# Moving loads between queues and waits in the prologue of a fused state-space and feed-forward kernel

## The chip, the cores and the metric

The kernel runs on one core of a Trainium2 chip. The metric is device time in microseconds (us), start to end of one execution; a run's number is the median of several executions. TensorE (PE) multiplies matrices, VectorE (DVE) and ScalarE (ACT) work on SBUF and PSUM, GpSimd (POOL) works on SBUF. SyncE (SP), ScalarE and GpSimd also issue DMAs, each into a queue of its own.

## The reference

Two stages. The first is a chunked linear recurrence over a sequence, for 4 batches and 8 heads, 768 tokens, head size 32 and state size 16; the second a bilinear feed-forward layer over its output, with model width 256 and inner width 1536.

```python
log_a = np.log(np.clip(a, 1e-06, 1.0))
for c in range(nc):                      # chunks of 32 tokens
    cum = np.cumsum(la, axis=-1)
    L = np.exp(cum[:, :, :, None] - cum[:, :, None, :]) * causal
    M = np.einsum('bhin,bhjn->bhij', Cc, Bc) * L
    y_intra = np.einsum('bhij,bhjd->bhid', M, xc)
    y_inter = np.einsum('bhin,bhnd->bhid', Cc, state) * np.exp(cum)[:, :, :, None]
    y[:, :, sl] = y_intra + y_inter
    state = decay_full * state + np.sum(Bx, axis=2)   # Bx = B x, decayed to the chunk's end
...
x = attn_out.transpose(0, 2, 1, 3).reshape(B * S, H * D)     # 3072 tokens x 256
return ((x @ w_a) * (x @ w_b)) @ w_out
```

Inputs and output are float32.

## The kernel before

**Tiling.** The kernel uses blocks of 128 tokens (six of them) instead of the reference's chunks of 32. A block has four batches, worked in two pairs, so there are twelve pairs p = 0 to 11; pairs 0 and 1 are block 0. VectorE's `scan` turns `a` into running products `Pr`, one block per instruction. Their value in the middle of the block is inverted (`over_mid`, tile `rmid`), and factors for B and C come from `Pr` and `rmid`: for block 0 by small matmuls (`factors_mm`), for blocks 1 to 5 by `mid_rows`, `turned_rows`, `batch_factors` and `batch_inverse`.

**One pair of block 0.** `scale_bc` multiplies B (tile `bm`) and C (tile `cm`) by their factors on VectorE. `transposes` turns both on TensorE, VectorE copies B out (tile `bt`), ScalarE copies C (tile `ct`). `scores` multiplies them into four PSUM banks, `mask` multiplies with the causal table (three quarters on VectorE, one through ScalarE and GpSimd), `pv_u` or `pv1` multiplies the masked scores with x, and the result goes to `X2T` as float16.

**Block 1 (pairs 2 and 3) and later blocks** have B and C loaded by batch (`load_q`, tiles `bq` and `cq`); `scale_q` scales them on GpSimd into `planes`, and `turn` transposes them on VectorE (tile `turned`) for `scores`. `clear` fills the planes with zeros once.

**Feed-forward.** `unit_mm` multiplies two inner columns' worth of weights `Wa` or `Wb` with `X2T`, `evac_a` copies the a-part to SBUF on ScalarE, `times` multiplies it with the b-part on VectorE. `out_mm` multiplies with `Wo`. From block 1 on, `bunit` and `bout` do the same for all four batches at once. Each weight matrix is loaded in two halves by GpSimd (`load_w`, `load_wo`), which converts float32 to float16 on the way.

**Order.** The schedule is written out by hand (`tc.manual_schedule()`): each engine runs its instructions in the order of the program text, and waits only where data or a buffer makes it wait. Feed-forward units stand between the steps of the recurrence so that TensorE has work. `warmup` matmuls, whose results nobody reads, fill TensorE's time in the first microseconds. PSUM banks for the feed-forward come from the string `BANKS`, one digit per call of `bank()`.

**Queues.** The first loads alternate between SyncE and ScalarE. GpSimd issues the x of pair 0, the first halves of Wa and Wb, the x of pair 1 and the second half of Wa in one go; Wb's second half follows later, and Wo's halves at lines 864 and 876. SyncE's loads of block 1 carry an explicit wait on the first half of Wa (tile `w0`, lines 815 and 816). Behind them on SyncE stand the float32 x of pairs 2 and 3 (`load_x32`) and their B (`load2`). `load1` (line 143) loads one batch of one pair, or a part of its partitions if `i0` and `n` are given.

Of the kernel before, what the change touches and what calls it, by code (L numbers as in the profile page):

```python
# [14 lines left out]
ALU = mybir.AluOpType  # L15
PSUM = bass.MemoryType.PSUM
AFTER = mybir.DependencyInfo(mybir.DependencyClass.Sync, mybir.DependencyReason.DATA)
# [2 lines left out]
SS = 64.0  # L20

BANKS = (
    "012313213212312312031203123021032103120312013201320130231021302130231203120312013023102310"
    "2312013201320132012301230123012301230123012301320132013201320132013201320132013201320"
)


# [1 line left out]
def kernel(  # L29
# [113 lines left out]
    def load1(eng, p, which, bt, i0=0, n=64, to=None):  # L143
        blk, bp = divmod(p, NBP)
        if p >= P2:
            return eng.dma_start(
                by_token(pair_in[p][which])[:, bt],
                (B, C, x)[which][2 * bp + bt, :, blk * Q : (blk + 1) * Q, :].rearrange("h q n -> q h n"),
            )
        src = (B, C, x)[which][2 * bp + bt, :, blk * Q + 2 * i0 : blk * Q + 2 * i0 + 2 * n, :]  # L150
        if to is None:
            to = pair_in[p][which]
        return eng.dma_start(
            to[64 * bt + i0 : 64 * bt + i0 + n].rearrange("i h r n -> i h (r n)"),
            src.rearrange("h (i r) n -> i h (r n)", r=2),
        )
# [3 lines left out]
    def load_q(eng, blk, parts=ALL_Q):  # L160
        if blk not in by_batch:
            by_batch[blk] = [inq.tile([128, H, 4, N], f32, name=n_, tag=n_) for n_ in ("bq", "cq")]
        return [
            eng.dma_start(
                by_batch[blk][w][32 * b : 32 * b + 32].rearrange("i h s n -> i h (s n)"),
                (B, C)[w][b, :, blk * Q : (blk + 1) * Q, :].rearrange("h (i s) n -> i h (s n)", s=4),
            )
            for w, b in parts
        ]
# [12 lines left out]
    def load_w(half, W):  # L182
        src = moe_w_a if W is Wa else moe_w_b
        c = slice(half * KC, (half + 1) * KC)
        return nc.gpsimd.dma_start(W[half], src.rearrange("(f p) e -> p f e", p=128)[:, :, c])

    def load_wo(half):
        return nc.gpsimd.dma_start(
            Wo[:, 6 * half : 6 * half + 6].rearrange("p (g kk) e -> p g (kk e)", kk=3),
            moe_w_out.rearrange("(g p kk) e -> p g (kk e)", p=128, kk=3)[:, 2 * half : 2 * half + 2],  # L190
        )
# [6 lines left out]
    load1(nc.scalar, 0, 1, 1)  # L198
    load1(nc.sync, 0, 1, 0, 0, 32)
    load1(nc.scalar, 0, 1, 0, 32, 32)  # L200
    for w in (1, 0):
        load1(nc.sync, 1, w, 0)
        load1(nc.scalar, 1, w, 1)
    nc.scalar.preload_act_table_set("natural_log_exp_and_others")
    nc.vector.memset(zero, 0.0)
    nc.gpsimd.memset(ident, 1.0)
# [21 lines left out]
    for p in range(2):  # L228
        for bt in range(2):
            load1(nc.gpsimd, p, 2, bt)  # L230
        if p == 0:
            w0 = load_w(0, Wa)
            load_w(0, Wb)
    load_w(1, Wa)

    def warmup(bank, *widths):
        for cols in widths:
            nc.tensor.matmul(  # L238
                bank[:, 0:cols],
                nc.const_aps.tensor(1.0, [128, 128], mybir.dt.bfloat16),  # L240
                nc.const_aps.tensor(1.0, [128, cols], mybir.dt.bfloat16),
                start=True,
                stop=True,
                skip_group_check=True,
            )


    def scan(lo, hi):
        for k in range(lo, hi):
            nc.vector.tensor_tensor_scan(Pr[:, k], a_sb[:, k], zero, 1.0, ALU.mult, ALU.add)  # L250

    def over_mid(lo, hi):
        nc.vector.reciprocal(rmid[:, lo:hi], Pr[:, lo:hi, 63])
# [32 lines left out]
    def mid_rows(lo, hi, eng):  # L286
        k = slice(lo + NBLK - NT, hi + NBLK - NT)
        eng.tensor_tensor(
            out=Ps[:, lo:hi], in0=Pr[:, k], in1=rmid[:, k].unsqueeze(2).broadcast_to((BH, hi - lo, Q)), op=ALU.mult
        )  # L290
# [5 lines left out]
    def turned_rows(lo, hi):  # L296
        nc.vector.transpose(
            Pt[:, lo:hi].rearrange("p k s c -> p (k s) c"), Ps[:, lo:hi].rearrange("p k (i s) -> p k s i", s=4)
        )
# [67 lines left out]
    def transposes(p, ps=None, between=None, apart=False):  # L367
        s = st[p]
        if ps is None and apart:
            ps = [SC[0], SC[1]]  # L370
        TB, TC = (TT[:, 0:256], TT[:, 256:512]) if ps is None else [t_.bitcast(f16)[:, 0:256] for t_ in ps]
        for T_, src in ((TB, s["bm"]), (TC, s["cm"])):
            for r in range(2):
                nc.tensor.transpose(
                    T_[:, r * 128 : (r + 1) * 128], src[:, r].rearrange("p h n -> p (h n)"), ident
                )
            if between:
                between()
                between = None
        BT = mid.tile([128, 2, 2, Q], f16, name="bt", tag="bt")  # L380
        CT = mid.tile([128, 2, Q], f16, name="ct", tag="ct")
        co, ci = CT.rearrange("p t q -> p (t q)"), TC
        if p < P2:
            co, ci = CT.rearrange("p t (i r) -> p r (t i)", r=2), TC.rearrange("p (r c) -> p r c", r=2)
        b_ = nc.vector.tensor_tensor(  # L385
            out=BT.rearrange("p e r k -> p e (r k)"),
            in0=TB.unsqueeze(1).broadcast_to((128, 2, 256)),
            in1=par.unsqueeze(2).broadcast_to((128, 2, 256)),
            op=ALU.mult,
        )  # L390
        c_ = nc.scalar.copy(co, ci)
        if apart:
            tc.declare_no_dep(c_.ins, b_.ins.name, reason="reads of two banks")
        if p < P2:
            BT = BT.rearrange("p e r (t i) -> p e r t i", t=2)
        s["BT"], s["CT"] = BT, CT
# [37 lines left out]
    def product0(m2, e):  # L434

        return (
            st[0]["T1"][:, 2 * m2 : 2 * m2 + 2].rearrange("p m (e r) q -> p e m (r q)", e=2)[:, e],
            (SC0, SC1)[m2][:, :, e * 256 : e * 256 + 256],
            causal.rearrange("p r q -> p (r q)").unsqueeze(1).broadcast_to((128, 2, 2 * Q)),
        )  # L440

    def mask(out_in, by_pool=False):
        o_, i_, c_ = out_in
        if by_pool:
            tmp = mid.tile([128, *c_.shape[1:]], f32, name="tmp", tag="tmp")
            nc.scalar.copy(tmp, i_)  # L446
            nc.gpsimd.tensor_tensor(out=o_, in0=tmp, in1=c_, op=ALU.mult)  # L447
        else:
            nc.vector.tensor_tensor(out=o_, in0=i_, in1=c_, op=ALU.mult)  # L449
# [110 lines left out]
    def evac0(u, bt, eng, py):  # L560
        o_, i_ = X2T[:, 0, bt, u], py[bt][:, u * Q : (u + 1) * Q]
        if eng is nc.scalar:
            nc.scalar.activation(out=o_, in_=i_, func=AF.Copy, scale=YS / SS)
        else:
            nc.vector.tensor_scalar(o_, i_, YS / SS, None, ALU.mult)
# [27 lines left out]
    def unit_mm(p, k2, W):  # L593
        ps = bank("aps" if W is Wa else "bps")
        for kk in range(2):
            k = 2 * k2 + kk
            for f in range(2):
                nc.tensor.matmul(  # L598
                    ps[:, kk * 2 * Q : (kk + 1) * 2 * Q],
                    W[k // 6][:, f, k % 6 // 3 * 384 : (k % 6 // 3 + 1) * 384].rearrange("p (c kk) -> p kk c", kk=3)[  # L600
                        :, k % 3
                    ],
                    X2T[:, p, :, f],
                    start=(f == 0),
                    stop=(f == 1),
                    skip_group_check=True,
                )
        return ps
# [175 lines left out]
    scale_bc(0, 1, nc.vector, v.rearrange("p (r b h) -> p r b h", r=2, b=NBP)[:, :, 0])  # L784
    over_mid(1, 2)
    sel_over_mid(1, 2, nc.vector)
    mid_rows(0, 1, nc.gpsimd)
    tb, tcp = bank("tb"), bank("tc")
    transposes(0, [tb, tcp], lambda: warmup(SC[3], 256))
    nc.scalar.copy(flat(fC, 0, 1), v)  # L790
# [3 lines left out]
    mask(product0(0, 0))  # L794
    mask(product0(0, 1))
    mask(product0(1, 1), by_pool=True)
    mask(product0(1, 0))
    clear(planes[0], nc.gpsimd)
    warmup(tcp, 512)
# [5 lines left out]
        evac0(0, bt, nc.scalar, py)  # L805
    warmup(tcp, 512, 128)
    scale_bc(1, 1, nc.vector)
    scan(4, 5)
    scale_bc(1, 0, nc.vector)
    clear(planes[1], nc.gpsimd)  # L810
    pv_u(0, 1, py, True)
    for bt in range(2):
        evac0(1, bt, (nc.scalar, nc.vector)[bt], py)
    load_w(1, Wb)
    for i_ in load_q(nc.sync, 1):
        tc.add_manual_dep(i_.ins, w0.ins.name, AFTER, reason="first weights ahead of block 1")
    for p in (2, 3):
        tiles(p)
    x_in = [load_x32(p) for p in (2, 3)]
    for p in (2, 3):  # L820
        load2(nc.sync, p, 0)
    warmup(tcp, 512, 512)
    transposes(1, apart=True)
    aps = [unit_mm(0, 0, Wa)]
    scan(5, NBLK)
    over_mid(2, NBLK)
    clear(planes[2], nc.gpsimd)
    nc.gpsimd.tensor_tensor(out=hr, in0=Pr[:, 0:NG, Q - 1], in1=rmid[:, 0:NG], op=ALU.mult)
# [32 lines left out]
    nc.scalar.copy(G.rearrange("p g k -> p (g k)"), gps)  # L861
    times(0, 2, bps[2], asb[2])
    turned_rows(0, 1)
    load_wo(0)
    batch_factors(0, 1, *range(nb), eng=nc.gpsimd)
    mid_rows(1, NT, nc.gpsimd)
    go((1, 0))
    batch_inverse(0, 1)
# [198 lines left out]
```

## Time and profile before

| | us |
|---|---|
| median of 3 runs | 122.73 (122.69 to 123.84) |
| the profiled execution | 122.69 |
| its span, first to last instruction | 120.8 |

| engine | busy us | share of the span |
|---|---|---|
| TensorE, matmuls | 115.9 | 96% |
| VectorE | 90.2 | 75% |
| TensorE, weight loads | 73.9 | 61% |
| ScalarE | 67.9 | 56% |
| GpSimd | 58.8 | 49% |

The profile gives times from the start of the span. Its engine names are those of the chip's parts: PE (matmuls), PEld (weight loads of TensorE), DVE, ACT, POOL, and SPq or ACTq for the DMA issues of SyncE and ScalarE. Each instruction has its line in the kernel; the line may be that of a helper. Numbers in brackets behind an instruction are the time that its engine was idle before it and what released it. TensorE's busy time includes the warmups and counts modelled ends of matmuls. DMA lines give packets, megabytes and the time that the packets took as a share of 16 engines, queue by queue: q0 is GpSimd's, q1 SyncE's, q10 ScalarE's. For a DMA issue, "us to landing" counts from issue to the last arrival.

### The profile page before, as it was taken

To read this page: it belongs to the slowest core of one execution; us is meant where nothing else is said; L and a number is where in the kernel's file an instruction comes from. 1 tells how busy PE (TensorE), PEld (TensorE's weight loads), DVE (VectorE), ACT (ScalarE), POOL (GpSimd) and SP (SyncE) were. 2 spreads that over 40 slices of the span, in tenths; PEclk is the share of its full clock that TensorE was granted. 3 is DMA by queue.
4 is the path that set the end of the run, shared out by engine and by line. 5 is a ranking of instruction groups with operands and counts; after the bars stand their busy time and mean duration, and the time that the engine had idled before them with its cause. 6 is when DMAs were issued, how large, how long until landed. Compare 5 with 4: busy or idle time off the path is not lost.

```text
span 120.8 us, 3551 instructions
## 1 busy us (share of the span) xinstructions
PE 115.9 (96%) x1385; PEld 73.9 (61%) x1386; DVE 90.2 (75%) x166; ACT 67.9 (56%) x136; POOL 58.8 (49%) x92
## 2 busy tenths in 40 slices
PE   7989999999999999999999999999999999999990
PEld 2436789888644488544485464775465684645880
DVE  5998988999798994599966999686899426758000
ACT  0446756769776646567666646635735637475230
POOL 7994986999699969387803994200000000000000
PEclk9999999999999999999999999999999999999999
DMA  3999999894789994959992929012001111010132
GB/s 63 135 183 192 207 230 197 134 200 113 99 94 161 115 139 101 110 68 121 218 241 89 85 9 121 5 46 87 5 6 40 43 49 44 0 43 0 43 108 71
DMA packets 59297, 12.13 MB, mean 100 GB/s; under 512 B 54480, under 2 KB 59216, under 8 KB 59280
## 3 DMA queue, kind: packets, MB, share of 16 engines
q0 software_dynamic: 20320, 3.80, 38.9%
q1 hardware_dynamic: 36432, 7.74, 34.8%
q10 hardware_dynamic: 2528, 0.36, 1.8%
q8 instruction: 11, 0.18, 0.7%
q14 instruction: 6, 0.05, 0.1%
HBM read 12.42 MB, written 3.15 MB: 129 GB/s over the span
## 4 chain that ended last, share of the span: by engine, by line
PE 92%; DVE 4%; issue 0%; ACT 0%
PE ops L693 22%; PE aps L667 22%; PE bps L667 21%; PE ops L637 5%; PE aps L598 4%; PE SC L404 4%; PE bps L598 3%; DVE t L449 3%; PE SC L238 3%; PE SC L473 2%; PE SC L536 1%; PE tc L238 1%; PE py L458 1%; PE SC L485 1%; DVE bt L385 1%
## 5 line engine op out<-in xcount | busy, mean ns | idle before, releaser
L612 ACT COPY asb<-aps 128x512 f32<-128x512 f32 x72 | 42.0, 587 | 17.2 <-PE aps L667 13.4
L679 DVE TENSOR_TENSOR hkb<-bps,asb 128x512 f16<-128x512 f32 x60 | 40.2, 687 | 12.7 <-ACT asb L612 11.1
L667 PE MATMUL aps<-XB,Wa 128*128 128x512 f16 x120 | 35.7, 379 | 0.0
L667 PE MATMUL bps<-XB,Wb 128*128 128x512 f16 x120 | 35.7, 379 | 0.0
L693 PE MATMUL ops<-Wo,hkb 128*128 128x256 f16 (+1 forms) x252 | 28.1, 268 | 0.0
L693 PEld LDWEIGHTS <-hkb 128*128 128x128 f16 x252 | 23.0, 98 | 3.8
L667 PEld LDWEIGHTS <-Wb 128*128 128x128 f16 x120 | 12.4, 103 | 13.6
L667 PEld LDWEIGHTS <-Wa 128*128 128x128 f16 x120 | 12.1, 103 | 11.7 <-issue 0.5
L449 DVE TENSOR_TENSOR t<-SC,causal_q 128x512 f16<-128x512 f32 x27 | 17.3, 681 | 2.4 <-PE SC L404 2.4
L705 ACT ACTIVATE osb<-ops 128x256 f32<-128x256 f32 (+1 forms) x20 | 7.6, 379 | 18.4 <-PE ops L693 18.4
L447 POOL TENSOR_TENSOR t<-tmp,causal_q 128x512 f16<-128x512 f32 x5 | 5.8, 1161 | 10.0 <-ACT tmp L446 10.0
L177 POOL DMA_DIRECT2D xn<-in_x_dram x8 | 9.5, 1192 | 0.0
L346 POOL TENSOR_TENSOR planes<-cq,FC 128x256 f16<-128x256 f32 x10 | 7.6, 775 | 2.2 <-DMA cq<-in_C_dram 2.1
L622 DVE TENSOR_TENSOR hk<-bps,asb 128x512 f16<-128x512 f32 x11 | 7.2, 672 | 0.9 <-ACT asb L612 0.8
L346 POOL TENSOR_TENSOR planes<-bq,FB 128x256 f16<-128x256 f32 x10 | 7.7, 772 | 0.4 <-DMA bq<-in_B_dram 0.4
L449 DVE TENSOR_TENSOR t<-SC,causal 128x512 f16<-128x512 f32 x11 | 7.0, 675 | 0.4 <-PE SC L404 0.3
L598 PE MATMUL aps<-X2T,Wa 128*128 128x256 f16 x48 | 6.8, 274 | 0.0
L446 ACT COPY tmp<-SC 128x512 f32<-128x512 f32 x10 | 5.9, 589 | 1.5 <-PE SC L404 1.1
L598 PE MATMUL bps<-X2T,Wb 128*128 128x256 f16 x48 | 6.6, 273 | 0.0
L558 ACT ACTIVATE XB<-SC 128x512 f16<-128x512 f32 (+1 forms) x9 | 4.6, 547 | 3.5 <-PE SC L501 2.4
L447 POOL TENSOR_TENSOR t<-tmp,causal 128x512 f16<-128x512 f32 x5 | 5.8, 1161 | 0.0
L637 PE MATMUL ops<-Wo,hk 128*128 128x256 f16 x48 | 5.8, 273 | 0.0
(101 smaller groups left out, 109.2 us busy)
## 6 DMA issues: line engine op xcount, KB each, us to landing
out_dram<-osb SPq DMA_DIRECT2D x23, 128.0 KB, 1.8
cq<-in_C_dram SPq DMA_DIRECT2D x20, 64.0 KB, 3.9
bq<-in_B_dram SPq DMA_DIRECT2D x18, 64.0 KB, 3.8
bn<-in_B_dram SPq DMA_DIRECT2D x8, 128.0 KB, 4.1
xn<-in_x_dram POOLq DMA_DIRECT2D x8, 128.0 KB, 5.9
Wa<-in_moe_w_a_dram POOLq DMA_DIRECT2D x2, 384.0 KB, 7.3
Wb<-in_moe_w_b_dram POOLq DMA_DIRECT2D x2, 384.0 KB, 7.9
Wo<-in_moe_w_out_dram POOLq DMA_DIRECT2D x2, 384.0 KB, 6.5
```

Source lines behind the costliest of these rows:

```text
L177: eng.dma_start(by_token(pair_in[p][which]).rearrange("p t h n -> p (t h) n"), src.rearrange("t h q n -> q (t h) n"))
L346: eng.tensor_tensor(out=plane[:, c0 : c0 + 4 * step].rearrange("p (j c) s -> p j s c", c=step)[:, :, :, 0:N], in0=by_batch[blk][which][:, ...
L447: nc.gpsimd.tensor_tensor(out=o_, in0=tmp, in1=c_, op=ALU.mult)
L449: nc.vector.tensor_tensor(out=o_, in0=i_, in1=c_, op=ALU.mult)
L598: nc.tensor.matmul(ps[:, kk * 2 * Q : (kk + 1) * 2 * Q], W[k // 6][:, f, k % 6 // 3 * 384 : (k % 6 // 3 + 1) * 384].rearrange("p (c kk) -> ...
L612: (nc.vector.tensor_copy if on_dve else nc.scalar.copy)(asb, a_ps)
L622: eng.tensor_tensor(out=s["hk"][:, 2 * k2 : 2 * k2 + 2, :].rearrange("p k q -> p (k q)"), in0=b_ps, in1=asb, op=ALU.mult)
L637: nc.tensor.matmul(o_ps[:, 0:d_model], hk[:, k, bt * Q : (bt + 1) * Q], Wo[:, k, :], start=(k == 0), stop=(k == NK - 1), skip_group_check= ...
L667: nc.tensor.matmul(t_, W[k // 6][:, f, k % 6 // 3 * 384 : (k % 6 // 3 + 1) * 384].rearrange("p (c kk) -> p kk c", kk=3)[:, k % 3], XB[:, b ...
L679: return lambda: nc.vector.tensor_tensor(out=s["hk"][:, k], in0=ps[1], in1=asb, op=ALU.mult)
L693: nc.tensor.matmul(o_ps[:, 0:w], hk[:, k, c * Q : (c + 1) * Q], Wo[:, k, cs], start=(k == 0), stop=(k == NK - 1), skip_group_check=True,)
L705: nc.scalar.activation(out=o_sb[:, 0:w], in_=o_ps[:, 0:w], func=AF.Copy, scale=1.0 / (YS * YS))
```

## The change

Five edits, all in the order of work; no operation is added to or taken from the computation.

- The second batch of pair 1's B moves from ScalarE's queue to GpSimd's, behind the x of pair 0 and ahead of the first weights. ScalarE's load of pair 1's C is cut into two issues of 32 partitions.
- The second half of Wa is issued behind the fourth mask of pair 0 on GpSimd and not in the first go. `mid_rows(0, 1)` moves behind the issue of Wb's second half.
- The scan of block 4 moves from between pair 1's C and B scaling to behind the evacuation of pair 0's result.
- Block 1's loads on SyncE wait for the last scan, and no longer for the first half of Wa; the text of these loads, and of the loads of pairs 2 and 3 behind them, moves below that scan.
- `load_wo(0)` moves behind `batch_factors(0, 1, ...)` on GpSimd.

`BANKS` has other digits.

```diff
 BANKS = (
-    "012313213212312312031203123021032103120312013201320130231021302130231203120312013023102310"
-    "2312013201320132012301230123012301230123012301230132013201320132013201320132013201320"
+    "012313123121321321032103213102130213201320123012301231032102310231032013201320123103210321"
+    "0320123012301230120312031203120312031203120312301230123012301230123012301230123012301"
 )
...
     load1(nc.scalar, 0, 1, 0, 32, 32)
-    for w in (1, 0):
-        load1(nc.sync, 1, w, 0)
-        load1(nc.scalar, 1, w, 1)
+    load1(nc.sync, 1, 1, 0)
+    load1(nc.scalar, 1, 1, 1, 0, 32)
+    load1(nc.scalar, 1, 1, 1, 32, 32)
+    load1(nc.sync, 1, 0, 0)
...
         if p == 0:
-            w0 = load_w(0, Wa)
+            load1(nc.gpsimd, 1, 0, 1)
+            load_w(0, Wa)
             load_w(0, Wb)
-    load_w(1, Wa)
...
     def scan(lo, hi):
         for k in range(lo, hi):
-            nc.vector.tensor_tensor_scan(Pr[:, k], a_sb[:, k], zero, 1.0, ALU.mult, ALU.add)
+            i_ = nc.vector.tensor_tensor_scan(Pr[:, k], a_sb[:, k], zero, 1.0, ALU.mult, ALU.add)
+        return i_
...
     sel_over_mid(1, 2, nc.vector)
-    mid_rows(0, 1, nc.gpsimd)
...
     mask(product0(1, 1), by_pool=True)
+    load_w(1, Wa)
     mask(product0(1, 0))
...
     scale_bc(1, 1, nc.vector)
-    scan(4, 5)
     scale_bc(1, 0, nc.vector)
     clear(planes[1], nc.gpsimd)
     pv_u(0, 1, py, True)
     for bt in range(2):
         evac0(1, bt, (nc.scalar, nc.vector)[bt], py)
+    scan(4, 5)
     load_w(1, Wb)
+    mid_rows(0, 1, nc.gpsimd)
+    warmup(tcp, 512, 512)
+    transposes(1, apart=True)
+    aps = [unit_mm(0, 0, Wa)]
+    last_scan = scan(5, NBLK)
     for i_ in load_q(nc.sync, 1):
-        tc.add_manual_dep(i_.ins, w0.ins.name, AFTER, reason="first weights ahead of block 1")
+        tc.add_manual_dep(i_.ins, last_scan.ins.name, AFTER, reason="third weights ahead of block 1")
     for p in (2, 3):
         tiles(p)
     x_in = [load_x32(p) for p in (2, 3)]
     for p in (2, 3):
         load2(nc.sync, p, 0)
-    warmup(tcp, 512, 512)
-    transposes(1, apart=True)
-    aps = [unit_mm(0, 0, Wa)]
-    scan(5, NBLK)
     over_mid(2, NBLK)
...
     turned_rows(0, 1)
+    batch_factors(0, 1, *range(nb), eng=nc.gpsimd)
     load_wo(0)
-    batch_factors(0, 1, *range(nb), eng=nc.gpsimd)
     mid_rows(1, NT, nc.gpsimd)
```

More of the change, by code (lines that the diff above doesn't have):

```diff
@@ L22 @@
 BANKS = (
-    "012313213212312312031203123021032103120312013201320130231021302130231203120312013023102310"
-    "2312013201320132012301230123012301230123012301320132013201320132013201320132013201320"
+    "012313123121321321032103213102130213201320123012301231032102310231032013201320123103210321"
+    "0320123012301230120312031203120312031203120312301230123012301230123012301230123012301"
 )
```

## The prediction

> **What bounds the kernel now.** I read the totals by engine first (TensorE 96% busy, VectorE 75%), then three stretches of the span, the chain that ended last between 8 and 15 us, the order of instructions there, and last the DMA queues by stretch. From here on "the first product" is block 0's pair 1 (`transposes(1)`, `scores(1)`, its masks, `pv1`), and all times are us from the span's start.
>
> The stretches (columns: stretch; sum; busy us of PE, PE's weight loads, VectorE, ScalarE, GpSimd; clock; DMA share; GB/s):
>
> ```profile
> 0.00:14.85 14.85, 13.28 (x213) 7.32 (x214) 12.31 (x35) 6.55 (x14) 12.22 (x27) 1.00 1.12 155
> 14.85:31.30 16.45, 16.41 (x312) 14.31 (x313) 15.18 (x30) 11.69 (x28) 13.96 (x25) 1.00 0.97 173
> 31.30:110.97 79.67, 79.64 (x792) 46.40 (x791) 61.66 (x101) 47.68 (x89) 32.65 (x42) 1.00 0.73 79
> ```
>
> From 14.85 to 110.97 TensorE is busy 96.05 of 96.12 us, with a granted clock of 1.00, in an order written out by hand. Nothing in the change takes work from it. So the end can move in two ways only: what comes before 14.85 gets shorter or longer, or a load that comes later makes a new hole in the gapless part. Before 14.85 some of TensorE's time is `warmup`, which is filler: there VectorE's chain decides. The chain in order of time:
>
> ```profile
> 9.21 0.47 PE py L458 x16
> 9.68 0.54 PE tc L238 x2
> 10.22 0.32 PE SC L374 x4
> 10.54 0.87 PE aps L598 x8
> 11.41 0.47 PE SC L404 x32
> 11.91 1.90 DVE t L449 x3
> 13.86 0.42 PE SC L458 x32
> ```
>
> The step that the change touches is at 10.22, the transposes of pair 1. The timeline shows what they wait for:
>
> ```profile
> 8.99 0.46 DVE L333 TENSOR_TENSOR cm<-cn,fC 128x256 f16<-128x256 f32 x1
> 9.37 0.41 DVE L250 TENSOR_TENSOR_SCAN Pr<-a_sb,zero 32x128 f32<-32x128 f32 x1
> 9.61 0.61 PE L238 MATMUL tc<-const-bfloat16-1.0 128*128 128x512 bf16 x2
> 9.70 0.39 DVE L333 TENSOR_TENSOR bm<-bn,fB 128x256 f16<-128x256 f32 x1
> 10.14 0.11 PEld L374 LDWEIGHTS <-bm 128*128 128x128 f16 x2 [0.42 <-DVE bm L333]
> ```
>
> A scan stands between `cm` and `bm`, and `bm` ends at 10.09. But ScalarE's half of that B was issued at 3.60 with 6.0 to landing: 9.60. So without the scan, `bm` could start at 9.60 and not before. The scan costs 0.1 of it, the load hides the rest.
>
> **The change, part by part.**
>
> *Scan behind the evacuation, B through GpSimd's queue.* The half of B goes behind the two x loads: issued at 4.07, since each of those takes 0.78 and the first starts at 2.51. Its own landing is not in the trace. The x loads right ahead of it, of the same 64 KB, took 3.6 and 3.9; the x loads of pair 1 behind two weight halves took 6.7. So it lands between 7.7 and 10.8; I take 8.0, as nothing large is ahead of it. `bm` then starts when `cm` ends, at 9.40 instead of 9.70. The transposes can't follow by the whole 0.30: the two 512-column warmups are ahead of them on TensorE, at 9.61. Two such matmuls issue in 0.43 (the chain has 0.43 for each two of 512 columns at L667), so TensorE is free at 10.04. They start at 10.04 instead of 10.14: **-0.10**. The evacuation (0.27) and the moved scan (0.41) then run from 9.79 to 10.4, before `bt` at 10.48 needs VectorE: no cost; if they overran, each 0.1 would come straight back. The `bt`, the last scan, `rmid` and the masks keep their order, so 11.91 becomes 11.81 and 13.86 becomes 13.76, if TensorE's two units between have their weights.
>
> The Trainium skill, page "DMA: Bandwidth & Descriptors", section "Issuing engine by pattern", speaks against this part: it gives plain loads to Sync and calls the hardware path generally faster. The trace says otherwise here (6.0 on ScalarE's queue against 3.6 and 3.9 on GpSimd's); by the rule the half would land beyond 9.6, and the gain would be gone.
>
> *The first weights behind one more issue.* Every GpSimd issue behind the B half goes back by one issue, 0.72 to 0.78. Wa's first half landed at 4.06+5.8 = 9.86 and is first loaded into TensorE at 10.32, so 10.22 after the gain. If landing follows issue, it comes at 10.6: a loss of 0.4, net +0.3. If the engines are the limit, it hardly moves: from 4 to 7 they carried 3543 packets, nearly all under 512 B, and the B half was among them before as well, only in another queue. At that rate, 1180 a us, these and the 130 that ScalarE's queue still had between 7 and 9 are through by 7.1, and none of them then runs beside the weights. That gives 9.9 to 10.1. I take this, since the share of busy DMA engines is full all through: **0**, with +0.4 kept. Wb's half landed at 11.8 and is needed at 12.05; `pv1` waits for masks anyway, so the first 0.2 of lateness there is covered.
>
> *Wa's second half behind the pair-0 mask, `mid_rows` later.* GpSimd's mask starts at about 7.85 instead of 8.01 (its input ends at 7.76), Wa's half 1 is issued at 9.0 instead of 6.83, Wb's at 10.0 instead of 9.40. The queue still has pair 1's x until 12, so both keep their places; first uses are 17.85 and 19.16, landings were 15.7 and 18.1. `mid_rows` (0.39) falls where GpSimd stood idle 1.49: **0**.
>
> *Block 1's eight loads behind the last scan.* SyncE waited for Wa and issued at 9.85. Behind the scan that becomes 11.5, and queued behind it are the x of pairs 2 and 3 and four B loads. What did those 1.65 us bring before? Packets, MB and share by queue (q0 GpSimd's, q1 SyncE's), from 10 to 13.5, from 13.5 to 15.5 and from 16 to 17.5:
>
> ```profile
> q0 software_dynamic: 1426, 0.68, 145.1%
> ...
> q0 software_dynamic: 242, 0.35, 96.5%
> q1 hardware_dynamic: 194, 0.05, 18.8%
> ...
> q1 hardware_dynamic: 1457, 0.35, 123.6%
> ```
>
> Nothing of block 1 moved until 13.5, some 200 packets until 15.5, and the bulk (2048 packets in all) from 16, when the weights were through. Asking later loses at most what moved before 16, about 340 packets, 0.35 us at 971 a us; and the output weights no longer cut in at 18. So I expect landings within 0.3 of before (C at 17.4 to 19.1, B to 20.5). What needs them:
>
> ```profile
> 21.34 0.58 DVE L359 STREAM_TRANSPOSE turned<-planes 128x384 f32<-128x384 f32 x1
> 21.98 0.48 PEld L404 LDWEIGHTS <-turned 32*64 32x64 f16 x32 [0.21 <-DVE turned L359]
> 23.78 0.32 PEld L637 LDWEIGHTS <-hk 128*128 128x128 f16 x3
> ```
>
> `scores(2)` starts 0.06 after `turned` ends: hardly any slack. But GpSimd's scaling waited 1.38 for C at 19.32, and that wait is where a shift of the other sign would appear. I take **0**; the bounds are 0 (no gain: the 0.21 is the usual pause when TensorE changes its tile, as it also stands elsewhere behind "issue") and +1.6.
>
> The same page of the Trainium skill, section "Queues, rings and completion order", has each DMA engine take packets from its queues in turn. The trace agrees for 13.5 to 15.5 (194 against 242), not for 10 to 13.5. By the rule alone, 1.65 us of share, some 160 packets, would be lost: 0.17 us of landing.
>
> *Output weights behind the factor copies.* GpSimd starts the copies at 15.72 instead of 15.86 (VectorE's rows end at 15.70) and issues Wo's first half at 16.68 instead of 15.11. With its 6.9 to landing that is 23.6; Wo's second half took 6.1, Wb's second 8.7, so 22.8 to 25.4. It is needed with the matmul at 23.89, then 23.79: **0**, with +1.6 at the far end. `mid_rows(1,NT)` ends at 18.5 instead of 17.94, inside the wait for C. The bank string mostly exchanges the names of two banks, and each next user comes after an evacuation that is done.
>
> **Sum**: -0.10 on the profiled execution, 122.69 (span 120.8 and 1.9 around it), which is also within 0.04 of the median 122.73: **122.6**.
>
> **The rivals.**
> 1. *Block 1 lands as much later as it is asked for.* Scaling starts at 21.0, `turned` ends at 23.6, TensorE stands 1.6 at 21.98: 122.6+1.6 = 124.2. For it: 0.06 of slack. Against: nothing moved in the first 3.6 us. It decides once the B rows land after 20.6. **0.2**.
> 2. *Wo is late*, by 0 to 0.6 when x of pairs 2 and 3 moves beside it: 122.9. For it: slack 0.2. **0.2**.
> 3. *The first weights follow their issue*: net +0.3, 123.0. **0.1**.
> 4. *The B half is late on GpSimd's queue*: at 10.8 `bm` ends 1.1 later, 123.8 (the skill's rule above goes this way). Against: 3.6 and 3.9 right ahead. **0.05**.
> 5. *It brings nothing*, the 0.1 lost in TensorE's order: 122.7. **0.1**.
>
> **How the numbers follow.** The forecast has 0.35. Low end: the largest gain, 0.3 of `bm`, if the warmups gave way, 122.4, and a little for the runs' own spread: 122.3. High end: rival 1, 124.3. A difference of 1%, 1.2 us, is about what a measurement of this kernel can tell. Slower by more: rival 1 and part of 4 and of 2 and 3 together, 0.25. Faster by more: no row gives 1.2 us, 0.05 for what no row shows. Within: 0.70.
>
> **What would show it.** Right: `bm` of pair 1 at 9.4, transposes near 10.04, `scores(1)` near 11.24, `pv1` at 13.76, and TensorE gapless from 14.75. Wrong: Wa loaded after 10.4; `turned` ending after 21.9; a hole at `scores(2)` or ahead of the first output matmul at 23.8.

## The result, and the profile after

| | before | after |
|---|---|---|
| median of 22 runs, us | 122.74 (122.43 to 123.84) | 123.46 (122.86 to 125.01) |
| ratio, with its 95% interval | 1 | 1.0047 [1.0028, 1.0067] |
| the profiled execution, us | 122.69 | 123.22 |
| its span, us | 120.8 | 121.5 |

The change makes the kernel slower by about half a per cent. 122.6 was forecast; the measured 123.46 lies inside the range and on the other side of 122.74. Behind the changed places, line numbers are 2 higher than in the kernel before. All ratios are taken against executions of the kernel before from the same session (their medians run from 122.71 to 122.91). They leave out slow executions, those over 1.5% above the fastest of their kernel, while the medians take in all, and the profiles of `a_b_on_sync` and `n_short_queue` come from slow executions, at a granted clock of 0.97 where the others had 0.995 to 1.00, so their instants are not compared with the rest.

The stretches of the profile after, cut at the same instants and with the same columns as in the prediction:

```profile
0.00:14.85 14.85, 13.04 (x196) 7.06 (x197) 11.60 (x33) 6.18 (x13) 12.07 (x28) 1.00 1.08 147
14.85:31.30 16.45, 16.43 (x356) 14.25 (x331) 15.19 (x31) 11.61 (x29) 14.59 (x24) 1.00 1.01 177
31.30:110.97 79.67, 79.64 (x800) 46.62 (x793) 61.66 (x101) 47.75 (x89) 32.78 (x42) 1.00 0.77 80
```

From 14.85 on TensorE is as gapless as it was: 96.07 of 96.12 us, at a clock of 1.00. So the long part has no new hole, and the loss lies ahead of 14.85. There TensorE has 0.24 less busy time than before, and it had less work done by then: matmuls that were before the cut are now behind it (356 instead of 312 in the second stretch). The chain that ended last, in order of time, says what came in between:

```profile
4.07 0.67 POOL bn L153
4.74 6.37 DMA Wa<-in_moe_w_a_dram
...
11.15 1.05 PE aps L600 x8
12.21 0.47 PE SC L406 x32
...
12.71 1.90 DVE t L451 x3
...
14.65 0.42 PE SC L460 x32
...
15.64 0.62 PE aps L600 x4
```

Before, this stretch of the chain was `pv_u`, warmup, transposes, unit. Now it is GpSimd's issues and a load: the moved half of B, and behind it Wa's first half, issued at 4.74 (4.06 before) and landed at 11.11. The unit that multiplies with it starts at 11.15 instead of 10.54, `scores(1)` at 12.21 instead of 11.41, `pv1` at 14.65 instead of 13.86. The timeline of the same stretch shows both halves of the story:

```profile
9.09 0.41 DVE L335 TENSOR_TENSOR cm<-cn,fC 128x256 f16<-128x256 f32 x1
9.42 0.42 DVE L335 TENSOR_TENSOR bm<-bn,fB 128x256 f16<-128x256 f32 x1
9.95 0.32 PEld L376 LDWEIGHTS <-bm 128*128 128x128 f16 x2
...
11.15 0.78 PEld L600 LDWEIGHTS <-Wa 128*128 128x128 f16 x8 [0.78 <-DMA Wa<-in_moe_w_a_dram]
```

The intended part works: `bm` follows `cm` at once, with no wait for its load, at 9.42 (forecast 9.40). Then the weight loads stand for 0.78 us, until Wa has landed. The DMA issues, before and then after, have Wa's first half so (columns: queue, operation, count, KB, us from issue to landing):

```profile
Wa<-in_moe_w_a_dram POOLq DMA_DIRECT2D x1, 384.0 KB, 5.8
```

```profile
Wa<-in_moe_w_a_dram POOLq DMA_DIRECT2D x1, 384.0 KB, 6.4
```

It was issued 0.68 later and took 0.6 longer on top.

The other place that the prediction watched, `scores(2)`, has no hole of its own; `turned` stands 0.63 later than before, and the first load of it 0.79 later, as the front is:

```profile
21.97 0.58 DVE L361 STREAM_TRANSPOSE turned<-planes 128x384 f32<-128x384 f32 x1
22.77 0.49 PEld L406 LDWEIGHTS <-turned 32*64 32x64 f16 x32 [0.20 <-DVE turned L361]
```

Two instants sum up nearly all of these kernels. **The front** is the first load of Wa in `go((1, 0))`, right behind the first product: 14.85 before, 15.64 after. `scores(2)` starts at 21.98 and 22.77: 7.13 behind the front in both. Where it starts later than that, the excess is a wait for `turned`, that is, for block 1. The experiments are read with these two.

### The profile page after: what moved, and what is told of

The parts are those of the page before. It is cut to its first block, busy times and chain, and to the rows that moved or that the text cites. A ratio compares the mean times of both kernels' runs of the same rounds, so it can differ in the third digit from the quotient of the medians.

```text
span 121.5 us, 3552 instructions
## 1 busy us (share of the span) xinstructions
PE 116.4 (96%) x1386; PEld 74.1 (61%) x1386; DVE 90.1 (74%) x166; ACT 67.9 (56%) x136; POOL 59.4 (49%) x93
## 3 DMA queue, kind: packets, MB, share of 16 engines
q0 software_dynamic: 20352, 3.87, 41.2%
## 4 chain that ended last, share of the span: by engine, by line
PE 86%; DMA 5%; POOL 3%; DVE 2%; issue 0%; ACT 0%; POOLq 0%
PE ops L695 22%; PE aps L669 22%; PE bps L669 21%; DMA Wa<-in_moe_w_a_dram 5%; PE ops L639 4%; PE aps L600 4%; PE SC L406 4%; PE bps L600 3%; PE SC L475 2%; DVE t L451 2%; POOL xn L153 1%; PE SC L538 1%; POOL causal L226 1%; PE SC L487 1%; POOL bn L153 1%; PE SC L514 0%
## 5 line engine op out<-in xcount | busy, mean ns | idle before, releaser
L681 DVE TENSOR_TENSOR hkb<-bps,asb 128x512 f16<-128x512 f32 x60 | 40.2, 686 | 12.7 <-ACT asb L614 11.1
L239 PE MATMUL SC<-const-bfloat16-1.0 128*128 128x512 bf16 (+3 forms) x13 | 5.3, 543 | 0.8 <-PEq L1054 0.8
```

Of the source, the lines that this page charges most:

```text
L681: return lambda: nc.vector.tensor_tensor(out=s["hk"][:, k], in0=ps[1], in1=asb, op=ALU.mult)
```

## The experiments

Two theories to begin with. S: what costs is the issue ahead of Wa on GpSimd, since everything behind it on that queue moves by one issue. Q: what costs is the 64 KB of B that now stand ahead of the weights in the queue. A third suspect is block 1's later request, which the prediction had as its first rival. In the recorded texts the theories have letters, some of which are explained only further down: A is S with nothing else at cost, and B puts the cost on the later edits; M is two separate delays, Wa at the front and block 1 at `scores(2)`, of which the later one sets the end; F is the front alone; R is that any reordering of these loads costs 0.3 to 0.6. A kernel named a_... is the changed kernel with one edit, one named b_... the kernel before with one edit; the diffs show that edit alone. "Wa" is the issue of its first half plus the time to landing.

| kernel | median us | ratio to before [95%] | Wa | front | `scores(2)` | excess |
|---|---|---|---|---|---|---|
| before | 122.74 | | 4.06+5.8 | 14.85 | 21.98 | 0 |
| after | 123.46 | 1.0047 [1.0028, 1.0067] | 4.74+6.4 | 15.64 | 22.77 | 0 |
| a_b_on_act | 123.09 | 1.0020 [0.9998, 1.0043] | 4.05+6.1 | 15.12 | 22.31 | 0.06 |
| b_b_on_pool | 123.19 | 1.0036 [1.0012, 1.0060] | 4.73+6.1 | 15.52 | 22.65 | 0 |
| b_scan_only | 123.0 | 1.0011 [0.9991, 1.0032] | 4.04+6.1 | 15.20 | 22.33 | 0 |
| b_weights_later | 122.97 | 1.0013 [0.9988, 1.0039] | 4.05+5.9 | 15.08 | 23.46 | 1.25 |
| a_small_issue | 123.38 | 1.0028 [1.0006, 1.0051] | 4.55+6.2 | 15.33 | 23.02 | 0.56 |
| a_b_on_sync | 123.67 | 1.0061 [1.0032, 1.0090] | 4.05+5.8 | | | |
| a_b_behind_wa | 123.21 | 1.0025 [1.0006, 1.0044] | 4.05+6.4 | 16.13 | 23.27 | 0 |
| a_b_first | 123.69 | 1.0058 [1.0032, 1.0084] | 4.72+5.2 | 14.71 | 23.50 | 1.66 |
| a_causal_behind | 124.17 | 1.0061 [1.0036, 1.0087] | 3.80+6.2 | 15.43 | 24.00 | 1.44 |
| b_block1_late | 124.28 | 1.0111 [1.0073, 1.0149] | 4.05+6.1 | 15.10 | 23.08 | 0.85 |
| b_block1_late_wo_behind | 122.81 | 1.0005 [0.9991, 1.0019] | 4.06+6.1 | 15.02 | 22.14 | 0 |
| a_block1_early | 123.51 | 1.0046 [1.0017, 1.0074] | 4.73+5.6 | 14.90 | 22.27 | 0.24 |
| a_b_first_block1_early | 123.31 | 1.0027 [1.0006, 1.0048] | 4.72+5.7 | 14.98 | 22.60 | 0.49 |
| a_both_undone | 122.95 | 1.0021 [1.0006, 1.0036] | 4.06+6.3 | 15.08 | 22.21 | 0 |
| n_short_queue | 124.81 | 1.0132 [1.0087, 1.0177] | 3.81+5.9 | | | |

The last four columns are from one execution each, the median from many, and that execution is not always a typical one. `b_b_on_pool` (123.96), `a_b_behind_wa` (123.71), `a_b_first` (124.06) and `b_weights_later` (124.04, these two in their longest execution) were profiled well above their medians, `a_block1_early` (122.87) and `b_block1_late` (123.72, its shortest) below. Most intervals of neighbours overlap, so the medians tell a few kernels apart, and a trace says how one execution ran.

### Which edit costs

**B's half back on ScalarE's queue, all else as changed.**

```diff
-    load1(nc.sync, 1, 1, 0)
-    load1(nc.scalar, 1, 1, 1, 0, 32)
-    load1(nc.scalar, 1, 1, 1, 32, 32)
-    load1(nc.sync, 1, 0, 0)
+    for w in (1, 0):
+        load1(nc.sync, 1, w, 0)
+        load1(nc.scalar, 1, w, 1)
...
-            load1(nc.gpsimd, 1, 0, 1)
```

> Theory A (the GpSimd issue ahead of the weights makes Wa's first half late, and nothing else costs): Wa's first half is issued at 4.06 again and lands by 10.0 on all engines, TensorE has no wait for Wa at 10.2, the first unit of go((1,0)) starts at 14.8 to 14.9, median 122.6 to 122.8. Theory B (the later edits cost: block 1 behind the scan, the second half of Wa and Wo later): stays at 123.3 to 123.6, with a hole in TensorE after 14.85.

123.09. Wa is issued at 4.05 again and TensorE waits for it no more. What takes its place is the load that the scan used to hide. The timeline of this kernel:

```profile
9.94 0.42 DVE L333 TENSOR_TENSOR bm<-bn,fB 128x256 f16<-128x256 f32 x1 [0.64 <-DMA bn<-in_B_dram]
```

`bm` waits 0.64 for B, the transposes start at 10.42, and the front is at 15.12: 0.52 of the 0.79 is won back in this execution. The median lies between what the two theories expected, and its interval overlaps that of the changed kernel (from 1.0028), so the medians alone don't show the gain. C's load is whole again here too, as the diff shows.

**The queue move alone, on the kernel before** (the diff above the other way round).

> The kernel before with the B half alone moved to GpSimd's queue ahead of the weights. Theory A: Wa's first half lands at 10.4 to 11.2 and TensorE waits for it, median 123.2 to 123.5. Theory B: 122.7, no wait for Wa beyond 0.2.

1.0036, with an interval clear of 1: this edit costs without any of the others. But in the profiled execution it costs at another place. Wa's second half is still issued in the first go here, so the one issue more pushes GpSimd's own work too. GpSimd's timeline, and the `pv_u` that waits for it:

```profile
7.50 0.77 POOL L185 DMA_DIRECT2D Wa<-in_moe_w_a_dram  x1
...
8.69 1.14 POOL L449 TENSOR_TENSOR t<-tmp,causal 128x512 f16<-128x512 f32 x1
...
9.88 0.30 PE L460 MATMUL py<-t,xn 64*32 64x128 f16 x14 [0.29 <-POOL t L449]
```

The mask runs at 8.69 instead of 8.01, the second `pv_u` waits for it until 9.88, the transposes follow at 10.81, and by then Wa (4.73+6.1) is there. In the changed kernel the issue is paid at Wa, here at the mask: at whichever of its followers is needed first. This execution (123.96) loses 0.52 more at a later `turned`, first loaded at 36.15, for which another block's B was late; that is no part of the front.

**The scan alone**, behind the evacuation, with B still on ScalarE's queue.

```diff
-    scan(4, 5)
     scale_bc(1, 0, nc.vector)
...
+    scan(4, 5)
     load_w(1, Wb)
```

> The kernel before with only the scan of block 4 moved behind the evacuation. Both theories: bm of pair 1 starts at 9.6, when its load lands, transposes of pair 1 at 10.05 to 10.14, median 122.6 to 122.75.

1.0011, not to be told from 1. `bm` waits for its load (0.59) until 10.02, later than the 9.6 that was expected, so by itself this edit has nothing to gain.

**The weights' edits alone**: Wa's second half behind the mask, `mid_rows(0, 1)` behind Wb's second half, `load_wo(0)` behind the factor copies, all on the kernel before.

> The kernel before with the weights' edits alone: Wa's second half behind the fourth mask, mid_rows behind Wb's second half, Wo's first half behind the factor copies. Both theories: no wait for any weight beyond 0.2, median 122.5 to 122.8; if Wo is late after all, a hole ahead of the first output matmul near 23.8 and up to 123.2.

1.0013, not to be told from 1 either, and no wait for a weight in the trace. These edits show no cost, as forecast. The excess of 1.25 in this execution is a late load of block 1: 15 of the 16 arrivals of its last B were there by 20.25, the last one at 21.82.

### The bytes or the issue

**A load of 1 KB that nobody reads, in the slot of B's half**, and B's half back on ScalarE's queue. Nothing is left out of the computation.

```diff
+    spare = const.tile([16, 16], f32, name="spare")
...
-            load1(nc.gpsimd, 1, 0, 1)
+            nc.gpsimd.dma_start(spare, a.rearrange("b h s -> (b h) s")[0:16, 0:16])
```

> The changed kernel with the B half back on ScalarE's queue and, in its place on GpSimd's, a load of 1 KB that nobody reads. Theory S (the slot: Wa's first half is issued 0.7 later, at 4.74, and the last DMA engine then takes it up late): one DMA engine lands Wa at 10.8 to 11.1, TensorE waits for it, median 123.2 to 123.6. Theory Q (the bytes of B queued ahead of Wa): Wa lands by 10.2, median 122.9 to 123.1 as without the B half there.

1.0028, and TensorE waits again. The timeline:

```profile
10.84 0.78 PEld L600 LDWEIGHTS <-Wa 128*128 128x128 f16 x8 [0.57 <-DMA Wa<-in_moe_w_a_dram]
```

1 KB of data brings most of the wait back (0.57 of 0.78). So a wait like this doesn't need the 64 KB; the slot is enough. That the bytes add nothing is not shown: this is one trace, and by its median the kernel (1.0028) is told neither from `a_b_on_act` (1.0020) nor from the changed kernel. This execution lost 0.56 more at `scores(2)`, where block 1 was late as well.

The same trace shows something else. B's half is on ScalarE's queue here, issued at 3.59 as in the kernel before, and yet it is quick (columns as above):

```profile
bn<-in_B_dram ACTq DMA_DIRECT2D x1, 64.0 KB, 4.2
```

In the seven other kernels that have it on this queue, with Wa issued at 4.04 to 4.06, it took 6.0 to 6.4. There ScalarE's queue still moved packets from 7.5 to 9.5 beside Wa's (85 in the kernel before, 77 in `a_b_on_act`); here it moved none. So the queue alone does not make this load slow. An earlier Wa beside it may; that was seen in one execution and not tried apart.

**B's half as the last of SyncE's first loads.**

```diff
-    load1(nc.scalar, 1, 1, 1, 0, 32)
-    load1(nc.scalar, 1, 1, 1, 32, 32)
+    load1(nc.scalar, 1, 1, 1)
     load1(nc.sync, 1, 0, 0)
+    load1(nc.sync, 1, 0, 1)
...
-            load1(nc.gpsimd, 1, 0, 1)
```

> The changed kernel with the B half as SyncE's last first load, nothing ahead of the weights on GpSimd. Theory A: Wa lands by 10.0, the B half by 9.4, transposes of pair 1 at 10.05 to 10.2, median 122.6 to 122.8. Theory B: 123.3 to 123.6.

1.0061, no better than what it was to mend. The wait of `bm`:

```profile
12.26 0.42 DVE L334 TENSOR_TENSOR bm<-bn,fB 128x256 f16<-128x256 f32 x1 [2.79 <-DMA bn<-in_B_dram]
```

In this execution the half, behind SyncE's other first loads and beside the weights, arrives at 12.2, some 4 us later than on GpSimd's queue (8.0). It is the longest of the twelve (127.43), so the size of the wait does not stand for the others.

**B's half between Wa and Wb on GpSimd's queue.**

```diff
-            load1(nc.gpsimd, 1, 0, 1)
             load_w(0, Wa)
+            load1(nc.gpsimd, 1, 0, 1)
             load_w(0, Wb)
```

> The changed kernel with the B half between Wa's and Wb's first halves on GpSimd's queue. Both theories: Wa, issued at 4.06, lands by 10.2; the B half lands behind it at 9.7 to 10.4, the transposes of pair 1 start at 10.2 to 10.8, median 122.7 to 123.1.

1.0025, a median just above the expected 122.7 to 123.1. No wait for Wa (4.05+6.4 = 10.4), but behind 384 KB of weights B comes late: `bm` waits 1.50, and the front is at 16.13. The slot ahead of Wa and the slot behind it both cost; one delays Wa, the other B.

**B's half ahead of pair 0's x**, so that the order of the queue changes but not the number of issues ahead of Wa.

```diff
+    load1(nc.gpsimd, 1, 0, 1)
     for p in range(2):
...
-            load1(nc.gpsimd, 1, 0, 1)
```

> The changed kernel with the B half ahead of pair 0's x on GpSimd's queue; Wa is issued at 4.74 as before. Theory S: one engine lands Wa at 10.8 to 11.1, median 123.2 to 123.6. Theory Q: the B bytes are through long before Wa, which lands by 10.2, median 122.6 to 122.8.

1.0058, and two surprises. Wa, issued at 4.72 as in the changed kernel, landed at 9.9, as Q had it, and nothing waited for it: that an issue at 4.7 always makes Wa late is wrong. The time is the one that S expected, though, and in the same order with block 1 early (below) Wa landed at 10.4, so this one trace does not decide for Q. And with the front at 14.71, the forecast's gain was there, but block 1 was not:

```profile
10.18 0.81 PEld L600 LDWEIGHTS <-Wa 128*128 128x128 f16 x8
...
20.69 1.36 POOL L348 TENSOR_TENSOR planes<-cq,FC 128x256 f16<-128x256 f32 x2 [2.31 <-DMA cq<-in_C_dram]
...
22.87 0.58 DVE L361 STREAM_TRANSPOSE turned<-planes 128x384 f32<-128x384 f32 x1 [1.74 <-POOL planes L348]
...
23.50 0.49 PEld L406 LDWEIGHTS <-turned 32*64 32x64 f16 x32 [1.86 <-DVE turned L361]
```

Read upward from the last line: TensorE waits 1.86 for `turned`, that for the scaling, and the scaling 2.31 for block 1's C. In the changed kernel's profiled execution block 1 was earlier: its last B landed at 20.14, here at 21.86. So this loss is not one that the late front hides there.

**Two causal tables behind the weights' issues.** GpSimd builds the causal tables ahead of its loads; here that work comes behind Wb's first half, so that all loads are issued about 0.9 earlier.

```diff
-    for bt in range(2):
-        v = causal[64 * bt : 64 * bt + 64]
-        nc.gpsimd.affine_select(...)
...
             load_w(0, Wb)
+            for b_ in range(2):
+                v = causal[64 * b_ : 64 * b_ + 64]
+                nc.gpsimd.affine_select(...)
```

> The changed kernel with the two selects of the causal table (0.86 of GpSimd) moved behind the issue of Wb's first half, so all of GpSimd's first issues come 0.86 earlier and Wa's at 3.9, the B half still ahead of it. Theory S: Wa lands by 10.0 on all engines, no wait, transposes of pair 1 near 10.05, the first go((1,0)) unit near 14.75, median 122.5 to 122.7. Theory Q: one engine still lands Wa at 10.6 or later, median 123.0 to 123.4.

Wa was issued at 3.80 and was in time (10.0), as S has it. The time that S expected did not come: 1.0061. Pair 0 was slower (second `pv_u` at 9.89, transposes at 10.52), and `scores(2)` lost 1.44 on top. Pair 0 was slower because its C came later, the last of it at 5.85 instead of 4.93 in the changed kernel; its `cm`, which ran at 5.26 there, waits:

```profile
5.93 0.42 DVE L335 TENSOR_TENSOR cm<-cn,fps 128x256 f16<-128x256 f32 x1 [0.58 <-DMA cn<-in_C_dram]
```

GpSimd's earlier loads, which come with the only edit here, are the likely cause; one trace shows it.

Taken over the profiled executions but `a_causal_behind` and the two set apart above: six in which Wa was issued between 4.55 and 4.74 had it at 9.9, 10.4, 10.4, 10.8, 10.8 and 11.1; the eight in which it was issued between 4.04 and 4.06 had it between 9.8 and 10.4. TensorE was ready for it at 10.2 in `a_b_first` and at 10.4 in the changed kernel. With an issue 0.65 later the mean landing is some 0.4 later, 10.6 instead of 10.1, and the spread 1.2 instead of 0.6.

### Block 1

**Block 1 behind the last scan, alone, on the kernel before** (the wait and the place of the loads in the text).

```diff
-        tc.add_manual_dep(i_.ins, w0.ins.name, AFTER, reason="first weights ahead of block 1")
+        tc.add_manual_dep(i_.ins, last_scan.ins.name, AFTER, reason="first weights ahead of block 1")
```

> The kernel before with block 1's wait alone moved from Wa's first half to the last scan. Theory M: front as before (14.85), cq lands 0.5 to 1.2 later than 19.1, TensorE stands 0.3 to 1.6 at scores(2), median 123.1 to 123.9. Theory F: 122.6 to 122.8.

1.0111, above what either theory expected: the dearest single edit, more than twice the whole change. The timeline of this kernel:

```profile
21.65 0.76 POOL L347 TENSOR_TENSOR planes<-bq,FB 128x256 f16<-128x256 f32 x1 [1.84 <-DVE hk L623]
...
23.08 0.48 PEld L405 LDWEIGHTS <-turned 32*64 32x64 f16 x32 [1.05 <-DVE turned L360]
```

The scaling of B starts at 21.65, 1.1 later than before (20.54), and TensorE waits 1.05. The profile names VectorE's `hk` as the releaser; the next kernel scales B at 20.50 while its `hk` runs from 20.14 to 21.43, so it can't be that. B's loads are issued from 14.54 to 16.59 and take up to 5.3, which puts the last near 21.4. C was no later; it was scaled at 18.44, before the edit at 19.32.

**The same, with `load_wo(0)` behind the factor copies.**

```diff
     turned_rows(0, 1)
-    load_wo(0)
     batch_factors(0, 1, *range(nb), eng=nc.gpsimd)
+    load_wo(0)
```

> The kernel before with block 1's wait on the last scan and Wo's first half behind the factor copies. Theory M with the output weights as what block 1 has to share with: without Wo's packets beside it block 1 lands by 20.7, TensorE stands 0 to 0.6 at scores(2), median 122.9 to 123.4. If Wo has nothing to do with it: 124.0 to 124.5 as with block 1's wait alone.

1.0005: the whole cost is gone, by an edit that moves nothing of block 1. The timeline of this kernel:

```profile
16.82 0.76 POOL L188 DMA_DIRECT2D Wo<-in_moe_w_out_dram  x1
...
20.50 0.78 POOL L347 TENSOR_TENSOR planes<-bq,FB 128x256 f16<-128x256 f32 x1 [0.29 <-issue]
...
22.14 0.49 PEld L405 LDWEIGHTS <-turned 32*64 32x64 f16 x32 [0.20 <-DVE turned L360]
```

Wo's first half is issued at 16.82; in `b_block1_late` it was at 15.36, in the midst of block 1's eight loads. With it out of their way `turned` runs at 21.34, the instant of before. So block 1's later request is free only where Wo stands behind; Wo behind without it is in `b_weights_later` and shows no cost.

**The changed kernel with block 1 early again** (waiting for Wa's first half), **and the same with B's half ahead of x.**

```diff
-            load_w(0, Wa)
+            w0 = load_w(0, Wa)
...
-        tc.add_manual_dep(i_.ins, last_scan.ins.name, AFTER, reason="third weights ahead of block 1")
+        tc.add_manual_dep(i_.ins, w0.ins.name, AFTER, reason="third weights ahead of block 1")
```

> The changed kernel with block 1's loads waiting for Wa's first half again and not for the last scan. Theory M (two separate delays, Wa's landing at the front and block 1's landing at scores(2), of which the later one sets the end): the front stays late, 123.0 to 123.3, and where Wa happens to land in time 122.6; scores(2) never waits for turned by more than 0.3. Theory F (only the front counts): no change against the changed kernel, 123.3 to 123.6.

> The kernel with the B half ahead of pair 0's x, whose front was in time (first unit of go((1,0)) at 14.71) and which stood 1.65 at scores(2), now with block 1 waiting for Wa only. Theory M: cq lands by 19.2, scores(2) starts at 21.8 to 22.0, median 122.4 to 122.7. Theory F: stays at 123.5 to 123.8.

1.0046 and 1.0027. The first recovers nothing of the changed kernel's 1.0047, so block 1's request is not what the change loses. The second is lower than `a_b_first` (1.0058), though the intervals overlap; its excess at `scores(2)` is 0.49 instead of 1.66. Its median is between what M and F expected, that of the first is in F's range.

**Both undone in the changed kernel**: B's half on ScalarE's queue (the first diff) and block 1 early (the last).

> The changed kernel with the B half back on ScalarE's queue and block 1 waiting for Wa's first half: of the change there remain the scan behind the evacuation, the second half of Wa behind the mask, and Wo behind the factor copies. Theory M (two delays, Wa at the front and block 1 at scores(2), the later one sets the end): both are gone, Wa lands by 10.2, block 1's last B by 20.4, median 122.6 to 122.9. Theory R (any reordering of these loads costs 0.3 to 0.6, whichever it is): 123.2 to 123.5.

122.95: Wa at 10.4, no hole anywhere, front at 15.08. The remainder of 0.2% against before is measurable; its profiled front is 0.23 late because pair 0 was 0.27 late in that execution (second `pv_u` at 9.48 instead of 9.21). `bm` waited 0.22 for its load, but TensorE had its warmups until then and shows no wait.

### An attempt at a faster version

B's half on GpSimd, with the issues ahead of Wa kept few: causal tables behind Wb, pair 1's x behind the mask, block 1 on Wa's first half.

```diff
-    for p in range(2):
+    for p in range(1):
         for bt in range(2):
             load1(nc.gpsimd, p, 2, bt)
...
     mask(product0(1, 0))
+    for bt in range(2):
+        load1(nc.gpsimd, 1, 2, bt)
```

> A version made from the runs: the B half stays on GpSimd ahead of Wa, but the two causal selects and pair 1's x move behind the first weights (the selects behind Wb's issue, x behind the fourth mask), so that Wa is issued at 3.9; block 1 waits for Wa's first half. Theory M: Wa lands by 10.0, transposes of pair 1 at 9.85 to 10.1, go((1,0)) at 14.65 to 14.8, scores(2) at 21.8 to 22.3, median 122.4 to 122.8. Theory R: 123.2 to 123.5.

1.0132, the slowest of all, and above what either theory expected. In its profiled execution, the longest of six (125.63), pair 0's `cm` waits 0.88 for C's load, and everything behind it is late, as with the causal tables above. No version here beats the kernel before; the nearest is `b_block1_late_wo_behind`, at the same time.

## Why the prediction was wrong, point by point

- **Where the end can move** (right). Only what lies before 14.85, or a new hole behind it: the loss is 0.79 at the front, and 0.7 at the end of the span.
- **Scan behind the evacuation, B through GpSimd's queue: -0.10** (right, and lost again). `bm` ran at 9.42 without a wait. From the second `pv_u` to the first load of Wa it was 1.11 before (9.21 to 10.32); in `a_b_first`, where Wa is in time, it is 1.01 (9.17 to 10.18). In the changed kernel TensorE was ready for Wa after 1.05 (9.32 to 10.37, the 11.15 less its 0.78 of wait). This load took 3.9 from issue to landing on GpSimd's queue and 6.0 and 6.3 on ScalarE's (before and `a_b_on_act`). The prediction read such a difference as one of the queues; that is not shown, since on ScalarE's queue it took 4.2 in `a_small_issue`, where Wa was issued 0.5 later. The Trainium skill's rule cited there ("DMA: Bandwidth & Descriptors", section "Issuing engine by pattern"), that plain loads belong on Sync, was taken to mean a landing beyond 9.6. On GpSimd's queue the half landed at 8.0; on SyncE's it landed at 12.2, in the longest execution of `a_b_on_sync`. So no run here tests the rule fairly.
- **The first weights behind one more issue: 0, with +0.4 kept** (wrong; this is the step that failed). I let the mean packet rate set the landing, 9.9 to 10.1, and kept 10.6 as the far end. It was 11.1, and TensorE waited 0.78. The term had the wrong quantity: a wait ends with the *last* of a load's arrivals, one for each of the 16 DMA engines. In the landing events of the changed kernel's trace 15 of 16 are there by 9.96, as the mean rate has it, and the last comes at 11.11; before, 15 were there by 9.61 and the last at 9.83. Rival 3 named this place, with a chance of 0.1 and a price of +0.3. But its rule, that landing follows issue, gives 10.6 and is not what the arrivals did: with an issue 0.68 later the eighth moved by 0.2 (9.37 to 9.57), the fifteenth by 0.35, the last by 1.28. Measured: 0.11 that pair 0 was late in this execution, 0.06 gained, 0.78 of wait, together 0.83 at the first load of Wa.
- **Wa's second half, Wb's, `mid_rows`: 0** (right: `b_weights_later`, 1.0013).
- **Block 1's loads behind the last scan: 0** (right in the changed kernel, where B was scaled at 20.55 against 20.54, for a reason that was named and not priced). "The output weights no longer cut in" stood there as an aside; it is the condition of the whole term. Without it the edit costs 1.0111. That this is nearly rival 1's price (124.28 against 124.2) is luck: rival 1 had all of block 1 land later, and here C did not, only the two loads of B that were issued behind Wo (20.61 and 21.44 instead of 20.10 and 20.33). The working by packets moved before 16 (0.35 us) is too small for that case: B was scaled 1.1 later. The turns between queues that the Trainium skill states ("DMA: Bandwidth & Descriptors", section "Queues, rings and completion order") gave 0.17, too small as well.
- **Output weights behind the factor copies: 0** (right). Wo's first half, issued at 17.45, took 4.8 and was there 2.3 before the first output matmul's load at 24.57. Rival 2 falls. So does rival 4: B's half was not late.

What is shown: B's half on GpSimd's queue ahead of Wa, together with the cut of C's load that goes with it, costs without the other edits (`b_b_on_pool`, with an interval clear of 1), and the scan alone, the weights' edits alone and block 1's request together with Wo's place show no cost (`b_scan_only`, `b_weights_later`, `b_block1_late_wo_behind`); an earlier request for block 1 wins nothing back (`a_block1_early`). In the two profiled executions the difference is TensorE's wait for Wa, and a 1 KB issue in the same slot brings such a wait too (`a_small_issue`).

What stays open: whether the bytes of B add to it; why one DMA engine is 1.2 us behind the rest in one execution and not in another (`a_block1_early` and `a_b_first` had Wa in time or nearly, with medians as slow as the changed kernel's); and, with one profile of each kernel, how often each wait decides in the 22 runs. In `a_b_first`, and by 0.24 in `a_block1_early`, where the front was in time, part of the loss came at `scores(2)` instead. In the changed kernel's own profile block 1 was in time, so a second delay behind the first is not shown there. That Wa's wait is all of the median's loss is therefore argued and not shown.

## What to carry to other kernels

A load is in when its slowest arrival is in: price it by the spread of landings over several traces and not by the mean rate of the queues, and do not lean on a slack (here 0.3) that is smaller than that spread. An added DMA issue is paid by everything behind it on that engine, masks as well as weights, and by whichever is needed first. The price of an edit can hang on another one: block 1's later request cost 1.1% with the output weights in its way and nothing without them.

## What the runs showed of the hardware that was not expected

- An issue's length on GpSimd depends little on its size: with 1 KB in the slot Wa was issued at 4.55, with 64 KB at 4.74, without either at 4.05, so 0.50 and 0.69 us for 64 times the bytes. A 384 KB half of Wa took 0.72, and the 128 KB loads of x of later blocks took 1.2 each.
- The moved 64 KB cost GpSimd's queue hardly any packets. The queues on the page of before, and then of after (packets, MB, share of 16 engines):

```profile
q0 software_dynamic: 20320, 3.80, 38.9%
...
q10 hardware_dynamic: 2528, 0.36, 1.8%
```

```profile
q0 software_dynamic: 20352, 3.87, 41.2%
...
q10 hardware_dynamic: 2016, 0.30, 1.4%
```

ScalarE's queue (q10) lost 512 packets, GpSimd's (q0) gained 32 for the same 0.06 to 0.07 MB. The 1 KB load of `a_small_issue` added 32 to q0 as well (20352). Whether the packets are why the half was faster there was not tried apart; on ScalarE's queue with its 512 packets it took 4.2 once.
- The last of a load's 16 arrivals can be far behind the fifteenth, on GpSimd's queue and on SyncE's: 1.15 us for Wa in the changed kernel against 0.22 before, and 1.57 for the last B of block 1 in `b_weights_later` against 0.06 in the changed kernel.
